# A Strassen feed-forward behind windowed attention: the written-out order of all engines, banks and buffers replaced by another one

## The chip, the cores and the metric

The kernel runs on one core of a Trainium2 chip. Its time is the device time of one launch in microseconds (us), and the median of several launches is what counts. TensorE is called PE here, its weight loads PEld, VectorE DVE, ScalarE ACT, GpSimd POOL and SyncE SP. POOL and SP do no arithmetic that matters in this kernel: POOL issues the loads, SP the stores and the transposes that the DMA engines make.

## The reference

Attention with a window of 96 keys and 8 global keys, biased by distance, feeds a two-layer network with a squared ReLU. There are 4 batches of 768 tokens, 8 heads of 64, and a hidden width of 2048.

```python
scores = scale * np.matmul(q, k.transpose(0, 1, 3, 2))
...
scores = np.where(keep, scores + bias[None], -1e9)
a = np.exp(scores - max); a = a / (sum(a) + 1e-09)
x = np.matmul(a, v).transpose(0, 2, 1, 3).reshape(B * S, H * D)   # 3072 x 512
h = x @ w_in                                                       # 512 x 2048
r = np.maximum(h, 0.0)
out = (r * r) @ w_out                                              # 2048 x 512
```

## The kernel before, in words

The 3072 tokens are 24 tiles of 128 (six to a batch), and two tiles make one of 12 blocks. A loop over tiles and a loop over blocks only describe operations: each gets a name, the engines it may run on, what it depends on and the function that emits it (class `Plan`). What is emitted, in which order, on which engine and in which memory, stands in a table of 1224 words, `ORDER`, which `Plan.run` walks from the first to the last. Each engine works through its own instructions strictly in the order of the table.

A word is a name, then possibly `@A` or `@V` (ACT or DVE, where the operation may run on either), `#2` (the second operation of that name), and after a colon the numbers, in hexadecimal, of the banks or buffers that it takes: the eight PSUM banks for an operation of PE, one of 16 buffers `buf` of 128x512 float32 for most others.

The names, with the line of the profile of the kernel before:

- `ld.q.1`, `ld.win.3.0`, `ld.wout.2`: the first 34 loads, all issued by POOL (L327); `load.9.1` loads queries and keys of tile 9 (two DMAs), `load.9.0` its values (one), by POOL too (L331). `gate.9` is a DVE memset of one column of a value buffer (L501), for which `load.9.0` waits, and which itself waits for the last readers of that buffer.
- `T.9`: the transpose of the queries and keys of tile 9, a DMA issued by SP (L557), from tile 8 on; for tiles 0 to 7 it is `tr` on PE (L531) and a copy `T`.
- `sc.9.0`: the scores (PE, L621, 16 matmuls; 8 for the first tile of a batch, 24 where two tiles share one operation). `exp` (ACT, L687), `mul` by the exponential of the bias (DVE, L712), `pv.9.0` and `pv.9.1` (PE, L774, 8 matmuls each, or 4), `norm.9` (DVE, a reciprocal at L808 and a product at L809, which writes `x`).
- `xT.9`: the transpose of `x`, a DMA issued by SP (L894) from tile 8 on, before that `trx` on PE and a copy.
- `xs.4.0` to `xs.4.2`: sums of quarters of `xT` of block 4 (DVE, L988). The first layer is a Strassen product, for each block and each half of the hidden width (`h.4.0`, `h.4.1`) seven products `p1` to `p7` of 8 matmuls (PE, L1019), with copies `u` out of PSUM in between (ACT at L450 or DVE), sums with ReLU `c` (DVE at L1064; `c21` is a plain ReLU, at L919 on ACT) and squares `q` (ACT at L1086 or DVE at L1088). Block 0 and half of block 1 are done the plain way (`s1`, L1140, `relu`, `sq`).
- `sum.4.0` to `sum.4.3`: sums of the squared hidden values (DVE, L1234). The second layer is again seven products for each block, `s2.4.p1.0` and so on, in pieces of 4 matmuls (PE, L1279), with copies `part` (ACT at L450 or DVE at L452), and `o` (DVE, L1354, or a copy), which fill an output buffer.
- `st.4.0`: the store of the first 128 rows of block 4 (SP, L1376).

Three queues set what can start when. PE runs its pieces in the order of the table, and each waits for its operands and for its bank to be read out. SP issues stores and transposes in the order of the table, so that a store stands still behind a transpose whose `norm` isn't done, whoever waits for the store's buffer. POOL issues loads in the order of the table in the same way: a load waits for the readers of the buffer that it fills, and all behind it wait too.

`Plan.run` does no more than this:

```python
for word in ORDER.split():
    word, _, banks = word.partition(":")
    name, _, letter = word.partition("@")
    name, _, nth = name.partition("#")
    o = byname[name][int(nth or 1) - 1]
    o["engine"] = self.ENGINES[letter] if letter else next(iter(o["engines"]))
    o["banks"] = [int(b, 16) for b in banks]
```

Of the kernel before, what the change touches and what calls it, by code (L numbers as in the profile page):

```python
# [57 lines left out]
tr.0.0:0 T.0.0@A E0.1 tr.1.0:1 T.1.0@A ld.k.1 tr.1.1:2 T.1.1 bias.1.0:0345 ld.q.1 tr.0.1:2 T.0.1 ld.q.2 ld.k.2  # L58
bias.0.0:16 tr.0.2:7 T.0.2@A sc.1.0 exp.1.1.1:0 sc.0.0 exp.0.1.0:1 exp.1.0.1 exp.0.0.0 exp.1.0.0:3 tr.1.2:7 T.1.2 ld.q.3
tr.0.3:2 ld.k.3 tr.1.3:7 T.0.3 gk.1 T.1.3 exp.1.1.0 ld.v.1 bias.2.0:2654 sc.2.0 exp.2.1.1:2 gk.2 ld.v.0 exp.2.0.1  # L60
exp.2.0.0:4 pv.1.0:01 pv.1.1 ones.6 norm.1:0 sc.3.0:3745 gk.3@A exp.3.1.1:0 ld.k.4 tr.1.4:2 ld.q.4 exp.3.0.0:3 T.1.4
tr.0.4:0 T.0.4 gv.1 exp.2.1.0 exp.3.1.0 pv.0.0:12 pv.0.1 norm.0:1 mul.3.0:1 exp.3.0.1 mul.3.1:5 sc.4.0:0536 exp.4.1.0:6
ld.v.2 pv.2.0:12 pv.2.1 gv.2 exp.4.0.1:3 exp.4.1.1 trx.0:4 ld.q.5 norm.2:1 gk.4 tr.0.5:7 T.0.5@A xT.0:0 trx.1:5 ld.k.5
tr.1.5:3 T.1.5@A mul.4.1:0 xT.1@A ld.v.3 pv.3.0:12 pv.3.1 norm.3:0 exp.4.0.0 mul.4.0:3 sc.5.0:3476 exp.5.0.1:5 exp.5.1.1
ld.win.1.0 trx.2:5 xT.2:1 ld.win.3.0 s1.0.1:0 trx.3:1 xT.3 gv.3 s1.0.1#2 relu.0.1:6 s1.0.3:6 s1.0.3#2 relu.0.3:1 E0.0
exp.5.1.0:2 s1.1.1:0 relu.1.1@V:4 ld.v.4 ld.win.6.0 ld.win.0.0 ld.win.0.1 pv.4.0:56 pv.4.1 ld.win.2.0 ld.win.2.1 ld.v.5
s1.0.6:4 exp.5.0.0 relu.0.6:0 s1.1.3:0 sq.0.1:0 mul.5.1:3 norm.4:0 s1.1.0:4 s1.0.0:5 ld.win.7.0 s1.0.2:6 ld.win.5.0
relu.1.0:6 relu.1.3:5 sq.0.3 s1.1.2:3 s1.0.0#2 gv.4 gate.9 mul.5.0:7 relu.1.2:2 isum.0.0 isum.1.0 isum.2.0 sq.1.1:1
xs.1.0:0 pv.5.0:01 trx.4:4 xT.4@A:2 sq.1.3 pv.5.1 norm.5:0 isum.3.0 s1.0.2#2 s1.0.0#3 s1.0.0#4 relu.0.0@V:5 xs.1.1
ld.win.4.0 isum.0.1 xs.1.2 s1.0.2#3 s1.0.2#4 s1.0.7:4 sq.1.0 h.2.0.p1:0 u.2.0.1:6 trx.5:5 xT.5 isum.1.1 isum.2.1  # L70
relu.0.2:4 relu.0.7:3 s1.0.5:1 sq.1.2 h.1.1.p1:3 u.1.1.1:7 h.1.1.p2:6 relu.0.5:2 gate.10 h.2.1.p2:4 h.2.1.p1:5 sq.0.0
h.1.1.p6 u.2.1.1:1 h.2.0.p2:1 s1.0.4:7 xs.2.0:1 xs.2.1 xs.2.2 gate.14 c.1.1.c11:8 sq.0.6 h.2.1.p6 ld.wout.1 u.1.1.2:7
relu.0.4:0 sq.0.2 u.2.1.2:5 h.2.0.p6 u.2.0.2:4 isum.3.1 h.1.1.p7 u.1.1.3:9 c.2.1.c11:a h.2.1.p5:7 ld.wout.3 ld.wout.0
ld.wout.2 wsum.0.0 c.2.0.c11:1 h.2.0.p5:4 h.2.1.p7 u.2.1.3:6 h.2.0.p7 wsum.1.0 wsum.3.0 h.1.1.p5:1 s2.0.p1.0:6 h.2.1.p4
s2.0.p2.0:2 c.2.1.c22:b h.1.1.p4 h.2.1.p3 sq.0.4 sq.0.5 c.1.1.c22:0 wsum.2.0 ld.wout.4 sq.0.7 sum.0.0:0 u.2.0.3:9
h.2.0.p4 c.2.0.c22:3 q.1.1.c11 c.2.1.c21:2 ld.wout.6 ld.wout.7 c.1.1.c21:8 ld.wout.5 s2.0.p1.1 c.2.0.c21:9 s2.0.p2.1
q.2.1.c21:2 q.1.1.c21 part.0.p1:0 s2.1.p2.0:3 h.1.1.p3 load.6.1 tr.1.6:0 wsum.0.1 tr.0.6:5 sum.0.1 wsum.1.1 c.2.1.c12:2
o.0.p2:8 h.2.0.p3 c.1.1.c12:5 s2.1.p2.1 sum.0.2 s2.0.p6.0 s2.0.p6.1 wsum.3.1 wsum.2.1 gate.11 c.2.0.c12:7 load.6.0
load.7.0 s2.0.p5.0 s2.0.p5.1 load.7.1 tr.0.7:1 tr.1.7:7 q.2.0.c22 q.2.1.c11 q.1.1.c22 part.0.p6:0 T.1.6@A s2.0.p7.0
s2.0.p7.1 s2.1.p1.0:0 s2.1.p1.1 q.2.1.c22 q.1.1.c12 sum.0.3 sum.1.0:1 q.2.0.c21 part.0.p7:1 o.0.p5:9 s2.0.p4.0 T.0.6@A  # L80
sum.1.1 q.2.1.c12 s2.0.p4.1 gate.12 o.0.p4@V part.1.p1:1 T.0.7@A load.8.1 q.2.0.c12 s2.0.p3.0 s2.0.p3.1 sum.1.2 o.0.p3
sum.2.0:0 sum.1.3 o.1.p2:7 T.1.7@A s2.1.p6.0 s2.1.p6.1 part.1.p6:0 sc.6.0:276154 s2.1.p7.0 load.9.1 q.2.0.c11 sum.2.1
exp.7.0.0:2 s2.1.p7.1 part.1.p7@V:1 exp.6.1.0:1 exp.6.0.0 mul.6.0:4 gk.7@A T.8 s2.1.p5.0 s2.1.p5.1 s2.1.p4.0 s2.1.p4.1
exp.7.1.0 mul.7.0:5 o.1.p5:1 exp.7.0.1:b exp.7.1.1 mul.7.1:2 sc.8.0:1276 exp.8.1.1:0 exp.8.0.0:a pv.6.0:45 pv.6.1
norm.6:0 exp.8.0.1 s2.1.p3.0 s2.1.p3.1 o.1.p3 sum.2.3 s2.2.p1.0:6 o.1.p4 pv.7.0:45 pv.7.1 norm.7:1 gk.8@A s2.2.p1.1
trx.6:0 xT.6:2 exp.8.1.0 mul.8.1:2 gv.7@A T.9 sc.9.0:2371 load.10.1 load.9.0 part.2.p1:0 s2.2.p6.0 trx.7:0 exp.9.1.0:5
s2.2.p6.1 xT.7 exp.9.0.1:b gk.9@A h.3.1.p1:3 u.3.1.1:0 part.2.p6:1 load.12.0 load.8.0 s2.2.p2.0:0 mul.8.0:4 pv.8.0:45
pv.8.1 h.3.0.p1:7 s2.2.p2.1 T.10 xs.3.0:1 xs.3.1 norm.8:1 xT.8:1 sum.2.2 exp.9.0.0 mul.9.0:2 h.3.1.p6 xs.3.2 o.2.p2:5
h.3.0.p2:4 exp.9.1.1 u.3.0.1:4 c.3.0.c11:a gv.8 h.3.0.p6 s2.2.p7.0 u.3.1.2:3 load.11.1 gate.16 s2.2.p7.1 h.3.1.p7
h.3.1.p5:4 u.3.0.2:6 h.3.0.p7 mul.9.1:4 u.3.1.3:c c.3.1.c22:b pv.9.0:12 pv.9.1 norm.9:0 u.3.0.3:d h.3.1.p4 q.3.0.c11:1  # L90
h.3.0.p4 c.3.0.c21:a q.3.0.c21 T.11 c.3.1.c21@V:4 h.3.1.p2:5 c.3.1.c11:c gv.9 h.3.1.p3 c.3.1.c12:a sc.10.0:3712
exp.10.1.1:0 exp.10.1.0:2 part.2.p7@V:0 h.3.0.p5:5 c.3.0.c22:3 s2.2.p5.0 s2.2.p5.1 o.2.p5:e h.4.1.p1:7 gate.13
exp.10.0.0 mul.10.0:d exp.10.0.1 mul.10.1:f q.3.1.c21 q.3.1.c11 h.3.0.p3 c.3.0.c12:4 s2.2.p3.0 load.10.0 pv.10.0:12
s2.2.p3.1 pv.10.1 norm.10:1 u.4.1.1:2 h.4.0.p1:3 s2.2.p4.0 gk.10@A s2.2.p4.1 sc.11.0:1254 gv.10 o.2.p3 q.3.0.c22 xT.9
q.3.1.c22 xs.4.0:1 xs.4.1 xs.4.2 q.3.0.c12 u.4.0.1:b q.3.1.c12 sum.3.2:0 sum.3.0 s2.3.p1.0:0 exp.11.0.0:4 exp.11.0.1:a
h.4.0.p6 exp.11.1.1 u.4.0.2:3 load.12.1 h.4.1.p6 s2.3.p1.1 h.4.0.p2:1 h.4.1.p2:5 c.4.0.c11:6 gate.17 u.4.1.2:f load.13.1
exp.11.1.0 h.4.1.p5:4 o.2.p4 h.4.0.p7 u.4.0.3:b st.1.1 T.12 part.3.p1:1 h.4.1.p7 u.4.1.3:1 h.4.0.p5:6 h.4.0.p4
c.4.0.c21:0 mul.11.1:c gate.15 mul.11.0:d sum.3.1 load.11.0 st.0.1 q.4.0.c21:2 pv.11.0:12 h.4.1.p4 c.4.0.c22:4 q.4.0.c22
c.4.1.c21:0 c.4.1.c22:d pv.11.1 s2.3.p6.0 norm.11:0 h.4.0.p3 s2.3.p6.1 part.3.p6:0 xT.10:2 T.13 c.4.0.c12:4 h.4.1.p3
gate.18 c.4.1.c12:3 q.4.1.c12 s2.3.p2.0:7 c.4.1.c11:1 s2.3.p2.1 s2.3.p7.0 s2.3.p7.1 q.4.1.c21 q.4.1.c11 o.3.p2:f  # L100
q.4.0.c11@V load.13.0 sc.12.0:546123 exp.12.1.0:1 s2.3.p5.0 s2.3.p5.1 exp.12.0.0 q.4.0.c12@V part.3.p7@V:1 s2.3.p4.0
exp.13.0.1:4 h.5.0.p2:5 sum.3.3 o.3.p5:6 mul.12.0:0 gk.13 exp.13.1.1 mul.13.1:3 st.1.0 xT.11 xs.5.0:1 xs.5.1 gate.20
exp.13.0.0:2 h.5.0.p1:2 u.5.0.1:1 exp.13.1.0 mul.13.0:4 s2.3.p4.1 pv.12.0:34 pv.12.1 norm.12:0 s2.3.p3.0 load.14.1 T.14
c.5.0.c11:2 xs.5.2 h.5.1.p1:6 h.5.0.p6 o.3.p4 u.5.1.1:0 u.5.0.2:7 s2.3.p3.1 o.3.p3 h.5.1.p6 load.15.1 T.15 xT.12:1
pv.13.0:01 h.5.0.p5:3 load.16.0 pv.13.1 norm.13:1 gv.13 u.5.1.2:c q.4.1.c22 h.5.0.p7 u.5.0.3:d c.5.0.c22:3 sum.4.0:0
sum.4.1 load.16.1 st.2.1 s2.4.p1.0:7 h.5.1.p7 u.5.1.3:1 s2.4.p1.1 part.4.p1:0 h.5.0.p4 c.5.0.c21:d sum.4.2 q.5.0.c21@V:1
sc.14.0:0154 exp.14.0.1:4 st.2.0 h.5.1.p4 gk.14 exp.14.1.0:b exp.14.1.1 exp.14.0.0 h.5.0.p3 c.5.0.c12:a h.5.1.p5:5
c.5.1.c22:e load.14.0 s2.4.p6.0 s2.4.p6.1 s2.4.p2.0:0 part.4.p6:1 c.5.1.c21:5 sc.15.0:3412 exp.15.0.1:1 exp.15.1.0:7
h.5.1.p3 h.5.1.p2:6 s2.4.p2.1 exp.15.1.1 mul.14.0:d mul.14.1:9 h.6.0.p2:4 c.5.1.c12:b pv.14.0:12 pv.14.1 gk.15@A T.16
s2.4.p7.0 s2.4.p7.1 o.4.p2:c s2.4.p5.0 c.5.1.c11:4 norm.14:0 q.5.0.c12 sc.16.0:1265 exp.15.0.0 mul.15.0:0 q.5.1.c12  # L110
load.17.1 part.4.p7:0 gate.22 q.5.1.c21 mul.15.1:b sum.4.3 xT.13 xs.6.0:1 exp.16.0.1:5 gv.14 xs.6.1 exp.16.0.0:1
exp.16.1.0 mul.16.0:7 s2.4.p5.1 o.4.p5:9 h.6.0.p1:3 h.6.1.p1:6 u.6.0.1:a c.6.0.c11:1 s2.4.p4.0 s2.4.p4.1 q.5.0.c22
# [1386 lines left out]
```

## Time and profile before

| what | value |
|---|---|
| three runs | 201.02, 201.80, 202.25 us; median 201.8 us |
| profiled execution | 202.63 us, of which the profile's span is 200.9 us |
| granted TensorE clock | 1.000 |
| DMA packets | 111713, 26.92 MB |
| first transposes by SP | issued from 49.1 us (queries and keys) and 63.6 us (`x`) on |
| last loads by POOL | issued at 138.2 us |

The span runs from the first to the last instruction that the profile shows; 1.7 us of the profiled execution lie outside. The profiled execution is 0.8 us above the median of the three runs. A row of the timeline gives start, length, engine, line, output and input, and in brackets how long the engine stood idle before and what ended it. In the chain of waits a DMA's row runs from its issue to its landing, and a row of PE from the start of its first matmul to the start of what comes next.

### The profile page before, as it was taken

Reading aid. Unit: us, or ns where it says so; the run is one execution under the profiler, and the core shown is the slowest. Engines: PE = TensorE matmul, PEld = TensorE weight load, DVE = VectorE, ACT = ScalarE, POOL = GpSimd, SP = SyncE. Lnnn points to the kernel's source line nnn. Section 1 sums busy time; section 2 is a strip of 40 time slices with the busy share of each in tenths; the row PEclk is TensorE's granted clock in tenths of the full one; section 3 lists DMA queues with packets and bytes.
Section 4 is the critical chain, followed back from the end, with each engine's and each line's share of the span. In section 5 each row is a group of like instructions: output and inputs, shape, how many; then the busy total and the mean of one; then the engine's idle time right before and its main releaser. Section 6 shows DMA issues by size and latency. Waiting matters only on the chain.

```text
span 200.9 us, 6834 instructions
## 1 busy us (share of the span) xinstructions
PE 189.5 (94%) x2808; PEld 170.2 (85%) x2808; DVE 175.5 (87%) x395; ACT 159.0 (79%) x331; POOL 75.3 (37%) x93
## 2 busy tenths in 40 slices
PE   7878999999999999999699998999998999999993
PEld 2666999999879989999589997998888989989882
DVE  8369899999999998999769996897998998999951
ACT  6699788999998699898399987658997698568320
POOL 8999774757458055428002922315000000000000
PEclk9999999999999999999999999999999999999999
...
GB/s 127 148 152 163 182 193 206 202 157 118 134 174 141 152 156 152 172 171 117 211 123 67 122 119 140 231 89 199 30 58 182 29 108 132 134 0 3 104 80 184
DMA packets 111713, 26.92 MB, mean 134 GB/s; under 512 B 103234, under 2 KB 108866, under 8 KB 111682
## 3 DMA queue, kind: packets, MB, share of 16 engines
...
## 4 chain that ended last, share of the span: by engine, by line
PE 49%; DMA 31%; POOL 7%; DVE 6%; ACT 2%; issue 2%; SPq 0%; DVEq 0%; POOLq 0%; ACTq 0%
PE bank L1279 24%; PE bank L1019 19%; DMA win<-in_moe_w_in_dram 8%; DMA xT<-x 6%; DMA wout<-in_moe_w_out_dram 5%; DMA out_dram<-buf 5%; POOL qk_first L327 4%; DMA qkT<-qk 3%; DMA qk<-in_k_dram 3%; PE bank L774 3%; PE bank L621 3%; POOL v L327 2%; DVE x L809 1%; ACT buf L450 1%; DVE hsum L1234 1%
## 5 line engine op out<-in xcount | busy, mean ns | idle before, releaser
L450 ACT COPY buf<-bank 128x512 f32<-128x512 f32 (+1 forms) x55 | 30.2, 569 | 14.1 <-PE bank L1019 6.5
L1279 PEld LDWEIGHTS <-hsum 128*128 128x128 bf16 x384 | 35.4, 98 | 4.4 <-DVE hsum L1234 0.4
L1279 PE MATMUL bank<-wsum,hsum 128*128 128x256 bf16 x288 | 38.0, 273 | 0.0
L1086 ACT ACTIVATE hs<-buf 128x512 bf16<-128x512 f32 x52 | 31.9, 639 | 4.9 <-DVE buf L1064 4.9
L1019 PEld LDWEIGHTS <-win 128*128 128x128 bf16 x504 | 30.9, 98 | 4.0 <-issue 3.1
L1019 PEld LDWEIGHTS <-qk_first 128*128 128x128 bf16 x504 | 30.8, 98 | 2.5 <-DVE xs L988 1.0
L687 ACT ACTIVATE buf<-bank 128x512 bf16<-128x512 f32 x56 | 31.2, 615 | 1.1 <-PE bank L621 0.9
L1064 DVE CUSTOM_DVE_ANT_0 buf<-bank,buf 128x512 f32<-128x512 f32 x41 | 28.0, 686 | 3.3 <-PE bank L1019 2.7
L1279 PEld LDWEIGHTS <-hs 128*128 128x128 bf16 x288 | 26.6, 98 | 3.0 <-issue 0.2
L1279 PE MATMUL bank<-wout,hs 128*128 128x256 bf16 x192 | 27.2, 273 | 0.0
L331 POOL DMA_DIRECT2D qk<-in_q_dram x18 | 15.9, 886 | 29.7 <-DMA qkT<-qk 24.8
L331 POOL DMA_DIRECT2D v<-in_v_dram x18 | 16.1, 897 | 28.1 <-PE bank L1279 14.6
L1019 PE MATMUL bank<-xT,win 128*128 128x128 bf16 x336 | 24.0, 219 | 2.4 <-ACT buf L919 1.6
L1019 PE MATMUL bank<-xs,qk_first 128*128 128x128 bf16 x336 | 24.2, 219 | 0.6 <-DVE xs L988 0.6
L687 ACT ACTIVATE early<-bank 128x512 bf16<-128x512 f32 x32 | 18.0, 604 | 1.0 <-PE bank L621 0.9
L809 DVE TENSOR_TENSOR x<-bank,rs 128x512 bf16<-128x512 f32 x24 | 16.6, 692 | 0.9
L331 POOL DMA_DIRECT2D qk<-in_k_dram x18 | 16.1, 894 | 1.6 <-DMA wout<-in_moe_w_out_dram 1.6
L1234 DVE TENSOR_TENSOR hsum<-hs 128x1024 bf16<-128x1024 bf16 (+1 forms) x26 | 16.4, 642 | 0.1
L1354 DVE TENSOR_TENSOR buf<-bank,part 128x256 f32<-128x256 f32 x32 | 13.2, 417 | 3.9 <-PE bank L1279 3.8
L450 ACT COPY part<-bank 128x256 f32<-128x256 f32 x30 | 11.2, 374 | 4.9 <-PE bank L1279 4.7
L919 ACT ACTIVATE buf<-bank 128x512 f32<-128x512 f32 x17 | 10.0, 608 | 4.9 <-DMA out_dram<-buf 2.8
L621 PEld LDWEIGHTS <-qkT 64*128 64x128 bf16 x352 | 10.1, 94 | 3.9 <-issue 2.5
...
## 6 DMA issues: line engine op xcount, KB each, us to landing
...
v<-in_v_dram POOLq DMA_DIRECT2D x24, 128.0 KB, 6.2
qk<-in_q_dram POOLq DMA_DIRECT2D x18, 128.0 KB, 5.5
qk<-in_k_dram POOLq DMA_DIRECT2D x18, 128.0 KB, 6.5
...
qk_first<-in_k_dram POOLq DMA_DIRECT2D x5, 128.0 KB, 4.7
```

The source lines that it names most:

```text
L327: ("ld",) + name, {"LD": t}, lambda e: nc.gpsimd.dma_start(out=dst, in_=src),
L331: nc.gpsimd.dma_start(out=dst, in_=src)
L450: nc.scalar.copy(dst, src)
L621: nc.tensor.matmul(out=tiles["sc", j, odd, g][:, at, :], lhsT=left[j - 1][half, pair, :] if kt else qkT[j % NKT][half, 1, pair, :], rhs=qk ...
L687: nc.scalar.activation(out=tiles[tag, j, g][:, odd], in_=tiles.pop(("sc", j, odd, g)).rearrange("p a c -> p (a c)"), func=Act.Exp, scale=s ...
L809: nc.vector.tensor_tensor(out=x.rearrange("p (b a) c -> p b a c", b=2), in0=po[:, :, :, :D], in1=rs.to_broadcast([P, 2, 4, D]), op=Alu.mult,)
L1019: nc.tensor.matmul(out=tiles["h", blk, g, bank][:, n], lhsT=left_[:, s, k], rhs=right_[:, k], start=opens and n == 0 and k == 0, stop=k == ...
L1064: nc.vector._custom_dve(TENSOR_ADD_SAT, out=hr, in0=src, in1=tiles.pop(("u", blk, g, i)), s0=float("inf"), s1=0.0,)
L1086: nc.scalar.activation(hs, hr, Act.Square)
L1234: nc.vector.tensor_tensor(out=t[:, i, h], in0=t[:, a, h] if isinstance(a, int) else half_a(blk, *a)[:, h], in1=t[:, b, h] if isinstance(b, ...
L1279: nc.tensor.matmul(out=tiles["acc", blk, bank][:, cols], lhsT=left_[:, s], rhs=right_[:, cols], start=first and s == 0, stop=s == NSTEP - ...
L1354: nc.vector.tensor_tensor(out=o_sb[:, cols], in0=tiles["acc", blk, bank][:, part], in1=tiles["part", blk, other][:, part], op=Alu.add,)
```

## The change

Only the table `ORDER` is replaced: the same 1224 words stand in another order, with other engines for some and other banks and buffers for most. It takes one line more, so that every line number of the kernel's body is one higher after the change. Nothing else in the file differs. Two lines of the diff, from the table's middle, stand for all of it:

```diff
-h.7.0.p2:4 c.7.0.c11:5 sum.6.0 u.8.0.1:d h.7.1.p4 c.7.1.c21:4 part.6.p1:0 h.8.1.p1:5 u.8.1.1:8 gate.21 xs.8.0:1 xs.8.1
...
+s2.5.p5.1 st.2.1 h.8.1.p1:2 q.7.0.c22 s2.5.p4.0 h.7.1.p3 o.6.p2:b gate.19 load.19.0 xs.8.0:1 xs.8.1 sum.6.1 u.8.1.1:e
```

On ACT, six `part` copies fewer stand (24 for 30) and five `xT` copies more (7 for 2); DVE has six `part` more and five `xT` fewer; the other exchanges are of at most five instructions each. Each engine's count of arithmetic is the same to within 10 instructions.

The first place is SP's queue around the two stores of block 2 (`out_dram<-buf`). `qkT` is written by the transposes of queries and keys, `xT` by those of `x`; the numbers are those of the buffers. Before, the two stores stand together behind `xT.12`, whose input `x_104` is made by `norm.12`:

```order
L557 DMA_TRANSPOSE qkT_85<-qk_69 128x8x128
L557 DMA_TRANSPOSE qkT_86<-qk_67 128x8x128
L894 DMA_TRANSPOSE xT_107<-x_104 128x4x128
L1376 DMA out_dram<-buf_127 128x512
L1376 DMA out_dram<-buf_118 128x512
L557 DMA_TRANSPOSE qkT_87<-qk_68 128x8x128
L894 DMA_TRANSPOSE xT_107<-x_105 128x4x128
```

After, from the transpose of tile 11's `x` on:

```order
L895 DMA_TRANSPOSE xT_108<-x_104 128x4x128
L558 DMA_TRANSPOSE qkT_86<-qk_67 128x8x128
L1377 DMA out_dram<-buf_116 128x512
L895 DMA_TRANSPOSE xT_107<-x_105 128x4x128
L558 DMA_TRANSPOSE qkT_87<-qk_68 128x8x128
L895 DMA_TRANSPOSE xT_107<-x_104 128x4x128
L558 DMA_TRANSPOSE qkT_88<-qk_69 128x8x128
L1377 DMA out_dram<-buf_125 128x512
```

One store of block 2 (`buf_116`) has moved ahead of `xT.12`; the other now stands 17 places further down, behind `xT.17`. The last row is a store of block 3.

The second place is DVE's queue from `norm.19` (the first row, which writes `x` of tile 19 into one of two buffers) to the first two sums of block 9 (the last two rows), which need the transposed `x` of tiles 18 and 19. L712 is `mul`, L1234 `sum`, L1354 `o`, L1088 `q`, L452 a copy. Before:

```order
L809 TENSOR_TENSOR x_104<-bank,rs 128x512
L712 TENSOR_TENSOR early<-early,E 128x1024
L1234 TENSOR_TENSOR hsum_114<-hs_110,hsum_114 128x1024
L1354 TENSOR_TENSOR early<-bank,part_132 128x256
L1234 TENSOR_TENSOR hsum_115<-hs_113 128x1024
L712 TENSOR_TENSOR buf_120<-buf_127,E 128x1024
L452 COPY qkT_83<-qkT_80 128x4x8
L1234 TENSOR_TENSOR hsum_115<-hsum_115,hs_113 128x1024
L988 TENSOR_TENSOR xs<-xT_106 128x2x256
L988 TENSOR_TENSOR xs<-xT_106,xs 128x256
```

After:

```order
L810 TENSOR_TENSOR x_105<-bank,rs 128x512
L713 TENSOR_TENSOR buf_117<-buf_119,E 128x1024
L1089 TENSOR_TENSOR hs_111<-buf_123 128x4x128
L453 COPY part_130<-bank 128x256
L1355 TENSOR_TENSOR buf_116<-bank,part_130 128x256
L713 TENSOR_TENSOR buf_119<-buf_128,E 128x1024
L1235 TENSOR_TENSOR hsum_115<-hs_111 128x1024
L713 TENSOR_TENSOR buf_128<-buf_123,E 128x1024
L989 TENSOR_TENSOR xs<-xT_106 128x2x256
L989 TENSOR_TENSOR xs<-xT_106,xs 128x256
```

Seven instructions stand between as before: four long ones, two short ones and a tiny copy have become five long and two short ones.

The third place is the end of POOL's queue, from the load of tile 19's values (`v_72`, the first row) on; that load waits for `gate.19`. `qk_67` to `qk_69` are the three buffers for queries and keys. Before:

```order
L331 DMA v_72<-in_v_dram 128x8x64
L331 DMA v_79<-in_v_dram 128x8x64
L331 DMA v_75<-in_v_dram 128x8x64
L331 DMA qk_69<-in_q_dram 128x8x64
L331 DMA qk_69<-in_k_dram 128x8x64
L331 DMA qk_68<-in_q_dram 128x8x64
L331 DMA qk_68<-in_k_dram 128x8x64
L331 DMA v_71<-in_v_dram 128x8x64
L331 DMA qk_67<-in_q_dram 128x8x64
L331 DMA qk_67<-in_k_dram 128x8x64
```

After:

```order
L332 DMA v_72<-in_v_dram 128x8x64
L332 DMA v_71<-in_v_dram 128x8x64
L332 DMA qk_68<-in_q_dram 128x8x64
L332 DMA qk_68<-in_k_dram 128x8x64
L332 DMA qk_67<-in_q_dram 128x8x64
L332 DMA qk_67<-in_k_dram 128x8x64
L332 DMA v_76<-in_v_dram 128x8x64
L332 DMA v_73<-in_v_dram 128x8x64
L332 DMA qk_69<-in_q_dram 128x8x64
L332 DMA qk_69<-in_k_dram 128x8x64
L332 DMA v_74<-in_v_dram 128x8x64
L332 DMA v_75<-in_v_dram 128x8x64
```

After, the queries and keys of tiles 19 and 20 stand ahead of that load and so are no longer in this piece; tile 21's (`qk_67`) stand fifth and sixth in it, where before they were ninth and tenth. `gate.19` itself has moved down DVE's queue: before, 93.8 us of PE's work stand ahead of it in the table, after the change 115.3 us. At the queue's front, the last four loads of `w_out` now stand behind tile 6's queries and keys, tile 8's ahead of tile 7's, and the values of tiles 6, 7 and 8, which were issued with them, behind tile 9's queries and keys.

More of the change, by code (lines that the diff above doesn't have):

```diff
@@ L57 @@
 ORDER = """
[L58 to L112, printed above, removed]
@@ new lines @@
+h.5.0.p5:3 q.5.1.c11:1 h.5.0.p4 s2.4.p2.0:0 gate.16 c.5.0.c22:f pv.14.0:56 pv.14.1 sum.4.2 norm.14:1 exp.15.1.0:5
+exp.15.0.0 gk.15@A s2.4.p2.1 sum.4.3 o.4.p2:3 h.5.0.p3 gv.14 c.5.0.c12:d s2.4.p7.0 q.5.0.c22 c.5.0.c21:1 mul.15.1:f
+q.5.1.c21 T.16 sc.16.0:5621 exp.16.1.0:6 s2.4.p7.1 part.4.p7@V:1 s2.4.p5.0 h.6.0.p1:6 exp.16.1.1:7 xT.13 exp.16.0.1
+h.6.1.p1:1 mul.15.0:8 s2.4.p5.1 o.4.p5:e load.17.1 T.17 xs.6.0:1 xs.6.1 s2.4.p4.0 pv.15.0:23 pv.15.1 norm.15:0
+h.6.0.p2:7 q.5.0.c21 exp.16.0.0 s2.4.p4.1 q.5.0.c12 u.6.1.1:5 gk.16@A xs.6.2 u.6.0.1:f c.6.0.c11:d h.6.1.p2:5
```

147 lines of the change are left out of this document (99 added, 48 removed).

## The prediction

> **What bounds the kernel now.** I read the page first, then busy times by stage, then what ended each engine's waits in the stages where PE falls back, then the chain of waits.
>
> ```profile
> span 200.9 us, 6834 instructions
> PE 189.5 (94%) x2808; PEld 170.2 (85%) x2808; DVE 175.5 (87%) x395; ACT 159.0 (79%) x331; POOL 75.3 (37%) x93
> ```
>
> PE is busy for 94% of the span, so its work, which the change leaves as it is, is the bound, and only its pauses can go: 200.9 - 189.5 = 11.4 us. By stage:
>
> ```profile
> 0.00:20.00 20.00, 16.11 (x235) 11.52 (x236) 13.93 (x52) 16.14 (x36) 19.01 (x27) 1.00 1.81 147
> ...
> 40.00:60.00 20.00, 19.70 (x266) 17.22 (x264) 19.72 (x41) 19.14 (x43) 11.35 (x14) 1.00 2.05 146
> ...
> 90.00:110.00 20.00, 17.75 (x293) 16.05 (x290) 17.27 (x40) 15.98 (x35) 5.29 (x7) 1.00 1.26 133
> 110.00:130.00 20.00, 19.12 (x312) 18.11 (x310) 17.33 (x36) 16.28 (x35) 9.06 (x12) 1.00 2.12 152
> ...
> 150.00:160.00 10.00, 9.45 (x168) 8.76 (x166) 8.97 (x21) 7.16 (x16) 0.00 (x0) 1.00 0.44 100
> ```
>
> (From the left: stage, its length, then busy time of PE, PEld, DVE, ACT, POOL, the granted clock, DMA.) The start costs PE 3.9 us, 40 to 60 us 0.3, 90 to 110 us 2.25, 110 to 130 us 0.9, 150 to 160 us 0.55. In the second of these rows DVE is full (19.72 of 20). The clock is 1.00 throughout. What stands behind the largest pause is in the timeline:
>
> ```profile
> 90.87 1.92 SPq L894 DMA_TRANSPOSE xT<-x  x1
> 92.88 1.01 SPq L1376 DMA_DIRECT2D out_dram<-buf  x2
> 97.86 0.69 DVE L1064 CUSTOM_DVE_ANT_0 buf<-bank,early 128x512 f32<-128x512 f32 x1 [0.96 <-DMA out_dram<-buf]
> 98.61 0.43 PEld L1019 LDWEIGHTS <-qk_first 128*128 128x128 bf16 x7 [0.66 <-issue]
> 100.13 0.60 ACT L919 ACTIVATE buf<-bank 128x512 f32<-128x512 f32 x1 [2.79 <-DMA out_dram<-buf]
> 100.78 0.43 PEld L1019 LDWEIGHTS <-win 128*128 128x128 bf16 x7 [1.69 <-issue]
> ```
>
> The two stores of block 2 are issued right after `xT.12` has been; DVE and then ACT stand still until they land, because they want to write into the stored buffers, and PE stands behind both, 0.66 + 1.69 = 2.35 us. The other pauses after the start have the same nature, a late DMA:
>
> ```profile
> 55.96 0.28 PEld L621 LDWEIGHTS <-qkT 64*128 64x128 bf16 x10 [0.55 <-DMA qkT<-qk]
> ...
> 122.92 0.43 PEld L1019 LDWEIGHTS <-win 128*128 128x128 bf16 x7 [1.05 <-issue]
> ...
> 151.84 0.43 DVE L988 TENSOR_TENSOR xs<-xT 128x512 bf16<-128x512 bf16 x1 [0.90 <-DMA xT<-x]
> 152.64 0.34 PEld L1019 LDWEIGHTS <-qk_first 128*128 128x128 bf16 x6 [0.83 <-DVE xs L988]
> ...
> 176.21 0.69 DVE L1064 CUSTOM_DVE_ANT_0 buf<-bank,buf 128x512 f32<-128x512 f32 x1 [0.16 <-DMA out_dram<-buf]
> ...
> 180.63 0.43 PEld L1019 LDWEIGHTS <-win 128*128 128x128 bf16 x7 [0.33 <-issue]
> ```
>
> They are `T.8` (0.55), `xT.16` (1.05), `xT.19` by way of `xs` (0.83) and the store of block 8 by way of `c` (0.33). The chain of waits gives their times from issue to landing, and PE's pieces:
>
> ```profile
> 42.52 6.51 DMA qk<-in_k_dram
> 49.11 6.80 DMA qkT<-qk
> ...
> 56.59 0.35 PE bank L774 x8
> ...
> 59.39 0.55 PE bank L621 x16
> ...
> 61.15 0.45 PE bank L1019 x8
> 61.59 0.44 PE bank L1279 x4
> 62.03 0.49 PE bank L774 x16
> ...
> 88.46 0.24 PE bank L774 x8
> ...
> 93.47 6.64 DMA out_dram<-buf
> ...
> 101.86 0.42 DVE buf L1354
> ...
> 102.96 0.22 DVE rs L808
> 103.20 0.69 DVE x L809
> 103.89 0.60 DVE early L712
> ...
> 111.22 0.34 DVE buf L1354
> ...
> 114.19 8.69 DMA xT<-x
> ...
> 147.59 4.15 DMA xT<-x
> ...
> 172.49 3.57 DMA out_dram<-buf
> ```
>
> From these I measure distances in the two tables: PE's work between the piece that makes a DMA possible and the first instruction that needs its landing, at 0.45 us for eight matmuls of the first layer, 0.44 for four of the second, 0.49 for a tile's `pv`, 0.55 for a tile's `sc`. Where such a distance is longer than the DMA's way, nothing waits.
>
> **The change, part by part.** Work and counts are the same, so only waits have a price.
>
> *Stores of block 2.* Before, the way from the last `pv` of tile 12 (88.46), which releases `xT.12`, to the landings is 9.4 us for the first store (97.86) and 93.47 + 6.64 - 88.46 = 11.65 us for the second. PE's work up to their first users is 10 x 0.45 + 4 x 0.44 + 0.49 + 0.55 = 7.3 us, and 1.4 us more for the second. So both wait, and PE loses 2.35 us. After, `st.2.0` stands behind `xT.11` with 11 pieces of the first layer, 15 of the second and about 2.1 us of others from `pv.11` to its buffer's next user, 13.6 us; `st.2.1` stands behind `xT.17` with 15 and 10 pieces, 11.2 us. These waits go: 2.35 us. What is late next is the store `st.3.0`, first behind `xT.15`: 13 x 0.45 + 5 x 0.44 + 0.49 + 0.55 = 9.1 us against 9.4. I take 0.3 us for it; the ends are 0 and the 2.35 of the same wait before.
>
> *`xT.16`.* PE's work from `pv.16` to `h.8.0.p1` was 13 x 0.45 + 6 x 0.44 + 0.49 = 9.0 us, and 1.05 were lacking; now it is 16 x 0.45 + 13 x 0.44 + 0.49 = 13.4. The 1.05 us go, with 3.4 to spare.
>
> *`xT.19`.* From `pv.19` to the first piece that reads `xs` it was 5.4 us (7 pieces of the second layer, 3 of the first, `sc`, `pv`), and is 5.8 (9, 3, `sc`). DVE has as much between `norm.19` and `xs.9.0` as before, and two instructions more ahead of `norm.19`. Of 0.83 us I let 0.5 go, between 0 and 0.83.
>
> *Block 8's store.* The 0.33 us go: `c.11.1.c11` now takes a buffer that no store has to free.
>
> *`T.8`, `T.9` and the loads around them.* How far apart POOL's loads are issued and how long transposes take to land, in the answers on `v` and on `qkT`:
>
> ```profile
> L331 POOL DMA_DIRECT2D v<-in_v_dram x18: 873/902/947, 36.2 to 136.5; - x18
> DMA to landing us min/median/max: 3.6/6.2/9.5
> ```
>
> ```profile
> DMA to landing us min/median/max: 3.2/5.3/9.0
> ```
>
> `T.8` was issued (49.11) when tile 8's keys had landed (42.52 + 6.51). Ahead of tile 8's queries and keys stood POOL's first 34 loads and 6 other rows; now it is the 34 and 3 others, so they come 3 x 0.9 = 2.7 us earlier. PE reaches `sc.8.0` 0.9 us of work earlier, and 0.55 were lacking: 1.25 us to spare, and the 0.55 go. `T.9` gains one row, 0.9 us, while its `sc` comes 0.2 + 0.55 us earlier; it showed no wait, but how little it had to spare the rows don't say. I take 0.3 us, with 0 and 0.55, `T.8`'s old wait, as ends. The values of tile 6 stand 9 rows further back, 8.1 us. They had 56.59 - (36.2 + 6.2) = 14.2 us to spare, so about 5 are left: nothing.
>
> [...]
>
> *The loads behind `gate.19`.* After the change, PE has 17.5 us of work between that gate and `sc.21.0`. In this time five rows of POOL (4.5 us), a load of keys and `T.21` have to pass:
>
> ```profile
> qk<-in_k_dram POOLq DMA_DIRECT2D x18, 128.0 KB, 6.5
> ```
>
> 4.5 + 6.5 + 5.3 = 16.3 us, 1.2 to spare at medians. `xT.18` (5.5 us of PE's work after `pv.18`, before 6.0) and `xT.22` (5.4, before 6.2) have less room too. For the three I take 0.4 us; the ends are 0 and, with the slowest transpose, 9.0 - 5.3 - 1.2 = 2.5.
>
> *The end.* `st.8.1` now stands behind the first store of block 11, and 3.1 us of PE's work later `o.11.p5` takes its buffer, while block 8's other store took 3.57 us to land. I take 0.3 us, from 0 to 0.5. The last pieces of PE, and the copy and the store after them, stand as before.
>
> *The start.* The same 34 loads, of the same sizes, stand in nearly the same order: nothing, give or take one row of POOL, 0.9 us.
>
> *Sum.* 2.35 + 1.05 + 0.5 + 0.33 + 0.55 = 4.8 us go, 0.3 + 0.3 + 0.4 + 0.3 = 1.3 us come: 3.5 us less. The profiled execution's 202.63 us (span 200.9 and 1.7 around it) becomes 199.1. It lies 0.8 us above the median of the runs, 201.8, which becomes 198.3.
>
> **The rivals.** *Half of it comes back as waits for DVE and ACT.* While PE stood, DVE caught up: from 90 to 110 us it was busy for 17.27 of 20 us, and with 2.35 us less it would be 98% full; from 150 to 160, 8.97 of 9.45. For it speaks that DVE's and ACT's work are the same in sum; against it, that from 40 to 60 us DVE was 99% full and PE lost only 0.3. If the gains in these two stages (2.85 us) are halved, 1.4 us come back: 199.7; if nearly all of it does, 201.
>
> *The loads behind `gate.19` are late.* POOL's whole end hangs on one DVE memset, with 12 rows behind it. If `T.21` needs its slowest 9.0 us and DVE comes to the gate 1 us late, PE waits 2.5 + 1.0 us instead of 0.4: 201.4. Against it speaks that few other loads are under way then.
>
> *DVE becomes the bound, and the kernel slower.* After the change DVE has, from the start of `sc.6.0` to that of `pv.8.0`, eight long instructions at 0.60 us, five short ones at 0.34, two `norm` at 0.22 + 0.69 and two tiny copies, 8.3 us, while PE has 8.8 us of work: 0.5 us of room in 9. The 0.60 and 0.34 are steps of the chain, where the next instruction starts before the one before it has ended; the lengths in the rows above are 0.69 and 0.42. If DVE has to wait for the end each time, it takes 8 x 0.09 + 5 x 0.08 = 1.1 us more, PE falls back by 0.6, and in nine blocks by 5.4: 203.7, and up to 207 where there is less room. For it speaks the full second row of the stages; against it that the steps were so short in the stage before, too. It decides once 3.5 us are lost, 0.4 in each block.
>
> *The change doesn't do what the tables show.* Excluded: there is no scheduler behind the table.
>
> **How the numbers follow.** The forecast, with its terms at other values of their ranges, has a chance of 0.54 and gives 196.5 to 199.7: at the low end 201.8 - 4.8, the 0.33 that `xT.19` may bring more, and 0.2 of the start's. The first rival has 0.2 (199.7 to 201, a fifth of it just below 199.8), the second 0.08 (about 201.4), the third 0.18 (203 to 207, a quarter of it below 203.8). A measurement of this kernel can tell about 1% from no change, here 2 us. So faster by over 1%, under 199.8: 0.54 + 0.04 = 0.58. Within 1%, up to 203.8: 0.16 + 0.08 + 0.04 = 0.28. Slower: 0.14. The range that is to hold the time 8 times in 10 leaves out most of the third rival and the lowest end: 196.6 to 203.0. The forecast's own is 196.5 to 199.7.
>
> **What would show it.** In the profile after, the rows of waits on `out_dram<-buf` between 90 and 125 us should be under 0.5 us together, and PE should hardly stand between 60 and 130 us; `T.8` and `xT.16` should land over 1 us before their users. If DVE stands for 0.5 us or more ahead of `xs` in block 9, or PE for `T.21`, the terms for these were too small. If PE waits for DVE or ACT in many places by 0.1 to 0.4 us, the first or third rival holds. The prediction is wrong if the start loses more than 4.8 us, or if PE's pauses after 20 us add up to more than 6 us.

## The result

| | median (lowest to highest), number of runs |
|---|---|
| before | 201.53 us (201.02 to 202.25), 4 |
| after | 199.30 us (198.62 to 201.74), 4 |
| before, later, on one chip with the next row | 201.23 us (197.83 to 207.06), 37 |
| after, later, same chip | 199.25 us (198.73 to 200.25), 12 |
| before, later, on the chip of `b_again`, `b_again2`, `b_st16` and `a_gate` | 200.99 us (199.08 to 202.94), 23 |
| before, later, on the chip of `a_back`, `a_part9`, `a_dve18` and `a_best` | 200.52 us (198.70 to 204.83), 29 |

The ratio of after to before is 0.9875, with a 95% interval from 0.983 to 0.992, that is 2.5 us less. The medians in the table differ by 2.2 us, and by 2.0 in the later series; 3.5 were forecast, and 199.3 us came where 198.3 was forecast. That ratio leaves out runs over 1.5% above the fastest of their kernel (one of after), which in the later series would drop 22 of the 37 runs of before on account of one run of 197.83 us and give 0.998 for the after and 0.992 for the moved stores, so medians of all runs are compared below. A difference of two such medians is known to about 0.8 us, by drawing the runs of each series anew at random: 2.0 for after may be 1.1 to 2.5.

### The profile page after: what moved, and what is told of

Its sections match the earlier page's. It is cut to its first block, busy times and chain, and to the rows that moved or that the text cites. A ratio compares the mean times of both kernels' runs of the same rounds, so it can differ in the third digit from the quotient of the medians.

```text
span 196.6 us, 6851 instructions
## 1 busy us (share of the span) xinstructions
PE 188.2 (96%) x2808; PEld 170.1 (86%) x2808; DVE 175.1 (89%) x396; ACT 161.2 (82%) x330; POOL 75.0 (38%) x93
## 4 chain that ended last, share of the span: by engine, by line
PE 83%; DVE 5%; DMA 4%; POOL 4%; issue 1%; ACT 0%; DVEq 0%; POOLq 0%
PE bank L1280 35%; PE bank L1020 32%; PE bank L1141 5%; PE bank L775 5%; PE bank L622 4%; POOL qk_first L328 3%; DMA v<-in_v_dram 2%; DMA xT<-x 2%; DVE x L810 1%; DVE buf L713 1%; PE bank L871 1%; PE bank L532 1%; DVE rs L809 1%; DVE v L453 1%; POOL v L328 0%
## 5 line engine op out<-in xcount | busy, mean ns | idle before, releaser
L1087 ACT ACTIVATE hs<-buf 128x512 bf16<-128x512 f32 x60 | 37.0, 648 | 6.5 <-DVE buf L1065 6.4
L688 ACT ACTIVATE buf<-bank 128x512 bf16<-128x512 f32 x72 | 40.0, 618 | 1.4 <-PE bank L622 1.0
L451 ACT COPY buf<-bank 128x512 f32<-128x512 f32 (+1 forms) x57 | 30.9, 564 | 11.5 <-PE bank L1020 6.1
L1065 DVE CUSTOM_DVE_ANT_0 buf<-bank,buf 128x512 f32<-128x512 f32 x46 | 31.0, 683 | 1.1 <-ACT buf L451 0.5
L713 DVE TENSOR_TENSOR buf<-buf,E 128x1024 bf16<-128x1024 bf16 x31 | 20.9, 681 | 1.1 <-ACT buf L688 1.1
L920 ACT ACTIVATE buf<-bank 128x512 f32<-128x512 f32 x22 | 13.1, 606 | 2.4 <-issue 1.0
L1355 DVE TENSOR_TENSOR buf<-bank,part 128x256 f32<-128x256 f32 x30 | 12.5, 419 | 1.8 <-PE bank L1280 1.7
L775 PE MATMUL bank<-v,buf 128*128 128x65 bf16 x296 | 13.4, 193 | 0.3 <-DVE v L453 0.3
```

Source lines behind the costliest of these rows:

```text
L451: nc.scalar.copy(dst, src)
L688: nc.scalar.activation(out=tiles[tag, j, g][:, odd], in_=tiles.pop(("sc", j, odd, g)).rearrange("p a c -> p (a c)"), func=Act.Exp, scale=s ...
L713: nc.vector.tensor_mul(at, tiles.pop(("esc", j, g)), bias)
L775: nc.tensor.matmul(out=po[:, hi, :], lhsT=tiles["at", j, g][:, odd, at * P : (at + 1) * P], rhs=v_sb[kj][:, h, :], start=(i == 0), stop=(i ...
L1065: nc.vector._custom_dve(TENSOR_ADD_SAT, out=hr, in0=src, in1=tiles.pop(("u", blk, g, i)), s0=float("inf"), s1=0.0,)
L1087: nc.scalar.activation(hs, hr, Act.Square)
```

## The profile after

The page of the kernel after the change:

```profile
span 196.6 us, 6851 instructions
...
PE 188.2 (96%) x2808; PEld 170.1 (86%) x2808; DVE 175.1 (89%) x396; ACT 161.2 (82%) x330; POOL 75.0 (38%) x93
```

The profiled execution took 198.62 us. By stage (length, then busy time of PE, PEld, DVE, ACT, POOL, the granted clock, the DMA engines' share; that share is the sum of the packets' times over the time of the 16 engines, so it can be above 1):

```profile
0.00:20.00 20.00, 15.28 (x220) 10.85 (x221) 12.63 (x44) 17.13 (x36) 19.18 (x28) 1.00 1.85 151
...
40.00:60.00 20.00, 19.92 (x273) 17.50 (x270) 19.31 (x42) 19.12 (x41) 11.40 (x13) 1.00 2.21 157
...
90.00:110.00 20.00, 20.00 (x351) 18.28 (x348) 19.13 (x44) 19.09 (x42) 6.13 (x7) 1.00 1.64 163
110.00:130.00 20.00, 20.00 (x299) 19.14 (x297) 19.33 (x43) 15.00 (x30) 4.38 (x6) 1.00 0.72 112
130.00:150.00 20.00, 19.95 (x295) 17.53 (x293) 19.07 (x41) 16.58 (x36) 6.11 (x7) 1.00 1.43 120
150.00:160.00 10.00, 9.92 (x166) 9.12 (x165) 9.55 (x19) 8.40 (x19) 0.00 (x0) 1.00 0.45 82
```

PE does not stand at all from 90 to 130 us, where it stood for 3.1 us, and from 20 to 180 us it stands for 0.25 us in all. The first 20 us cost it 4.72 us instead of 3.89. What it waits for, over the whole span (us in total, times, longest), are now things of the start:

```profile
PE bank L871 <- DVE x L810: 1.3, 2, 0.8
...
PE bank L622 <- DVE qkT L453: 0.5, 1, 0.5
PE bank L532 <- DMA qk_first<-in_k_dram: 0.5, 1, 0.5
PE bank L775 <- DMA v<-in_v_dram: 0.5, 1, 0.5
```

In the timeline, the two stores of block 2 (86.19 and 120.70, SP), the product on DVE that takes the first one's buffer (94.86), and what is left of the wait for tile 19's transpose (147.17 on DVE; at 147.98 PE's weight loads stand for 0.32 us, its matmuls for 0.05):

```profile
86.19 0.90 SPq L1377 DMA_DIRECT2D out_dram<-buf  x1
...
94.86 0.68 DVE L713 TENSOR_TENSOR buf<-buf,E 128x1024 bf16<-128x1024 bf16 x1
...
120.70 0.57 SPq L1377 DMA_DIRECT2D out_dram<-buf  x1
...
147.17 0.43 DVE L989 TENSOR_TENSOR xs<-xT 128x512 bf16<-128x512 bf16 x1 [0.25 <-DMA xT<-x]
...
147.98 0.45 PEld L1020 LDWEIGHTS <-qk_first 128*128 128x128 bf16 x8 [0.32 <-DVE xs L989]
```

The first store landed at 93.3, 1.5 us before DVE needed its buffer; `mul` starts there without a wait. `out_dram<-buf` is no longer among what DVE or ACT wait for between 60 and 190 us.

## The experiments

Theory 1 was the prediction's: PE's work is the bound and each wait has a price of its own. Theory 2: DVE and ACT use PE's pauses to catch up, so that about half comes back. Theory 3: DVE is the bound. Each edit is one of the table; the name of a kernel begins with `b` for the order before, `a` for the order after. Times are medians.

### The two orders again

`b_again` and `b_again2` are the order before, `a_again` is the order after, unchanged.

> The order before once more, unchanged, for a second profile: which of the pauses of 2.35 (stores of block 2), 1.05 (tile 16's x), 0.83 (tile 19's x), 0.33 (store of block 8) and 0.55 us (tile 8's queries and keys) come again. If they belong to the order, all five within 0.3 us. If some are chance of the execution that was profiled, those of the stores and of tile 19 stay and the others shrink, as they did beside the moved stores, where tile 8's transpose had 2.3 us to spare and tile 16's cost 0.2.

> The order before a third time, for one more profile. The same two readings: five pauses within 0.3 us of those shown, or the two of the stores and of tile 19 alone.

> The order after once more, unchanged, for its time beside the other runs on one chip and for a second profile. If the profiled execution shown is typical: PE's pauses in the first 20 us between 4.4 and 5.0 us, and under 0.6 us together from 20 to 180 us; the median of the runs 199.2, 2.3 below before. If the gaps of that profile are chance, they stand elsewhere.

The two executions of before took 202.82 and 200.14 us, with spans of 201.0 and 198.4. Their stages, `b_again` first:

```profile
90.00:110.00 20.00, 17.73 (x269) 15.86 (x267) 15.79 (x36) 14.64 (x31) 3.58 (x6) 0.91 1.71 121
110.00:130.00 20.00, 18.77 (x309) 17.81 (x307) 16.96 (x35) 16.11 (x35) 8.68 (x10) 1.00 2.15 150
...
150.00:160.00 10.00, 10.00 (x173) 9.32 (x171) 9.59 (x22) 7.30 (x17) 0.00 (x0) 1.00 0.54 105
```

```profile
90.00:110.00 20.00, 18.80 (x319) 16.93 (x316) 18.83 (x42) 17.11 (x38) 7.85 (x9) 1.00 1.16 130
110.00:130.00 20.00, 18.83 (x294) 17.95 (x293) 16.63 (x34) 15.94 (x34) 8.81 (x11) 1.00 1.83 155
...
150.00:160.00 10.00, 10.00 (x169) 9.24 (x167) 9.86 (x22) 7.76 (x17) 0.00 (x0) 1.00 0.51 118
```

In `b_again` the stores cost 2.27 us again and `xT.16` 1.23. In `b_again2` the stores landed in time (the later at 96.47), but tile 16's queries and keys came 1.2 us late instead, and `xT.16` cost 1.17. The pauses for `T.8`, `xT.19` and the store of block 8 are gone in both. In the profile that the prediction was made from they are 0.55, 0.83 and 0.33 us by PE's weight loads, which the prediction took, and 0.30, 0.55 and 0.15 by its matmuls. So two of the five pauses came again at their places, though not the stores' in every execution, and three were of that one execution. Neither reading of the expectations held: tile 19's went with the small ones, and tile 16's `x` stayed. From 20 to 180 us PE stood for 4.1, 3.5 and 2.5 us in the three profiles of before.

`a_again` (199.25 us) shows the same picture as the first profile of after, with 4.06 us of pauses in the first 20 us (4.4 to 5.0 were expected), and 0.5 from 20 to 180, nearly all of it at `xT.19`.

### The stores alone

```diff
-T.15 xT.12:1 ... load.16.1 st.2.1 ... exp.14.0.1:4 st.2.0
+T.15 st.2.1 st.2.0 xT.12:1 ... load.16.1 ... exp.14.0.1:4
```

> The order before, with one edit: the two stores of block 2 stand ahead of the transpose of tile 12's x instead of behind it. Theory 1 (PE's work is the bound, each wait has its own price): the 2.35 us that PE stood for these stores go, and the store's waits vanish from DVE's and ACT's rows between 97 and 101 us: 201.5 - 2.35 = 199.2. Theory 2 (DVE and ACT use PE's pauses to catch up): about half comes back as waits of 0.1 to 0.4 us: 200.3. Theory 3 (DVE is the bound): no change, 201.5.

It took 198.99 us (198.40 to 199.88, 12 runs) beside 201.23: 2.24 less. Theory 1 said 2.35. That it is met to 0.1 us is partly luck, since the difference may be 1.4 to 2.9 us; but theories 2 (1.2 less) and 3 (nothing) lie outside that, and fall at this place.

```profile
90.00:110.00 20.00, 19.69 (x339) 17.86 (x337) 19.57 (x43) 18.60 (x39) 9.09 (x11) 1.00 1.66 153
110.00:130.00 20.00, 19.99 (x306) 19.08 (x303) 17.68 (x35) 16.03 (x33) 7.28 (x9) 1.00 1.87 158
```

From 90 to 110 us DVE is now busy for 19.57 of 20 us and PE loses only 0.3 (to tile 17's queries and keys, which came 0.5 us late). `xT.16`, not touched, costs under 0.2 us here; why it shrank from 1.2, the runs don't show. Two words moved thus bring as much as the whole new order, and take most of the scatter away too.

### All five pauses, and the second one alone

`b_five` adds four edits to these stores, `b_st16` only the second of them:

```diff
-h.8.0.p1:1 h.7.1.p3 ... h.7.0.p4 load.22.0 s2.6.p1.1 s2.5.p5.1
+h.7.1.p3 ... h.7.0.p4 load.22.0 s2.6.p1.1 h.8.0.p1:1 s2.5.p5.1
...
-q.8.0.c21 h.9.1.p6 h.9.0.p6 s2.7.p3.1 part.8.p1@V:3 s2.8.p6.0
+q.8.0.c21 s2.7.p3.1 part.8.p1@V:3 s2.8.p6.0 h.9.1.p6 h.9.0.p6
...
-s2.9.p1.1 part.9.p1:1 s2.8.p3.1 o.8.p3 st.8.0
+s2.8.p3.1 o.8.p3 s2.9.p1.1 part.9.p1:1 st.8.0
...
-load.6.1 ... load.6.0 ... load.7.0 ... load.7.1 ... load.8.1
+load.6.1 load.7.1 load.8.1 ... load.6.0 ... load.7.0
```

> The order before, with five small edits, one for each pause that was named: the stores of block 2 ahead of tile 12's transpose; the first product of block 8 three pieces of PE later (tile 16's transpose); two products of block 9 two pieces later (tile 19's); block 8's last output piece one piece earlier (its store); tile 7's and 8's queries and keys ahead of the values of tiles 6 and 7 (tile 8's transpose). Theory 1: the pauses of 2.35, 1.05, 0.83, 0.33 and 0.55 us go, 5.1 together: 201.5 - 5.1 = 196.4. Theory 2: half comes back: 199.0. Theory 3: not below 200.5.

> The order before with the two moved stores, and the first product of block 8 three pieces of PE later (the second of the five edits alone). If the wait for tile 16's x has a price of its own, up to 0.2 us (what PE showed there beside the moved stores) less than 199.0: 198.8. If moving a piece on PE out of the way of a wait only sets up later waits, and that is where the five edits lost 0.95 us: 199.3 to 199.9.

`b_five` took 199.94 us: 0.95 more than the stores alone (it may be 0.3 to 1.8), 3.5 more than theory 1 said and 0.9 more than theory 2. Three of the five pauses were of one execution, so the four added edits had little to gain in any case. `b_st16` took 199.27 (beside a before of 200.99 on its chip), within the noise of the stores alone, so it can't tell whether the wait for tile 16's `x` still had a price of 0.2 us. PE's waits in `b_five` from 105 to 155 us, each behind what it waited for:

```profile
124.87 0.59 ACT L450 COPY buf<-bank 128x512 f32<-128x512 f32 x1 [1.45 <-DMA out_dram<-buf]
...
125.51 0.61 PE L1019 MATMUL bank<-xs,qk_first 128*128 128x128 bf16 x8 [0.23 <-ACT buf L450]
...
149.50 0.41 DVE L452 COPY part<-bank 128x256 f32<-128x256 f32 x1
...
149.96 0.60 PE L1279 MATMUL bank<-wsum,hsum 128*128 128x256 bf16 x4 [0.55 <-DVE part L452]
...
151.68 0.61 PE L1019 MATMUL bank<-xs,plain 128*128 128x128 bf16 x8 [0.23 <-ACT buf L450]
```

beside the one large one of `b_stores` in block 9:

```profile
148.72 1.07 PE L1019 MATMUL bank<-xs,qk_first 128*128 128x128 bf16 x16 [0.53 <-DVE xs L988]
```

The product that waited for `xs` has gone, and so has the wait for the transpose: DVE starts its sums `xs` at 147.95 without standing for it. PE now stands 0.55 us for a copy on DVE, `part.8.p1`, whose bank the next piece of PE needs. That piece has moved up on PE, but on DVE the copy still stands behind those sums and `norm.20` and ends at 149.91. The two smaller waits are for copies on ACT, and the first of these copies had itself waited 1.45 us for a store, a wait of 0.21 us in `b_stores`. From 20 to 180 us PE stands for 1.33 us in `b_five` and 0.85 in `b_stores`, in the first 20 us for 3.98 and 3.58, which together is about the 0.95 us, by one profile each. So a piece that moves on PE alone can set up a wait for another engine's queue; which of the four edits costs what, these runs don't separate.

### The late store put back

```diff
-T.15 st.2.0 xT.12:1 exp.14.1.0 mul.14.1:3
+T.15 xT.12:1 st.2.0 exp.14.1.0 mul.14.1:3
```

> The order after, with one word moved: the first store of block 2 stands behind the transpose of tile 12's x again, as before the change, instead of one place ahead of it. It will be issued at about 90.6 us instead of 86.2 and land 7 us later, at 97.7, while the product on DVE that takes its buffer starts at 94.9: DVE stands for 2.8 us. Theory 1 (a late store is what the kernel before paid for): PE stands for about 2 us there, 199.2 + 2.0 = 201.2, and the runs scatter more than after's. Theory 2 (the order after has slack in DVE that takes it up): within 0.5 us of after, 199.2 to 199.7.

199.29 us (198.86 to 201.19), where `a_again` took 199.25 on another chip; across chips 0.6 us can't be told. PE does not stand at all from 90 to 110 us in its profile (20.00 us busy), so nothing was lost at this place. The store was issued as expected, but was not late:

```profile
90.49 1.17 SPq L1377 DMA_DIRECT2D out_dram<-buf  x1
...
94.81 0.69 DVE L713 TENSOR_TENSOR buf<-buf,E 128x1024 bf16<-128x1024 bf16 x1
```

It landed at 94.72, 4.2 us after its issue instead of 7.1, 0.1 us before DVE took the buffer. The price that was expected was wrong, and the experiment doesn't tell the theories apart: the store was never late, so a late store's price is shown in the order before only. It shows that a store issued 4.3 us later landed only 1.4 us later.

### More work for DVE

```diff
-part.4.p6:2 ... part.5.p1:2 ... q.6.0.c12 ... q.7.0.c12
+part.4.p6@V:2 ... part.5.p1@V:2 ... q.6.0.c12@V ... q.7.0.c12@V
```

> The order after, with nine copies of the second layer's products (blocks 4 to 8) moved from ACT to DVE, at their places: 9 x 0.42 = 3.8 us more for DVE at most (3.1 by the steps of 0.34), as much less for ACT. From 60 to 180 us DVE is idle for 7.2 us after the change. Theory 1 (DVE has this room, PE stays the bound): less than 1 us more, 199.2 to 200.2. Theory 3 (DVE is the bound already): all of it, 202.3 to 203.0.

> As the kernel with nine copies moved, and nine squares of the first layer (blocks 4 to 9, 0.60 to 0.68 us each) moved from ACT to DVE too: 8.5 to 9.9 us more for DVE between 60 and 180 us, where 7.2 are idle. Theory 1: what exceeds the room is paid, 1.3 to 2.7 us, and some more where the room lies in other stages: 201 to 203. Theory 3: 207.7 to 209.

With nine copies moved 201.17 us (200.46 to 202.12), with nine squares as well 206.40 (206.17 to 206.65): 1.9 and 7.1 us more than `a_back` on the same chip. (In the edit, the first two words of each line stand for the nine copies, the last two for the nine squares.) The pages, nine copies first:

```profile
PE 190.4 (95%) x2808; PEld 171.2 (86%) x2808; DVE 177.5 (89%) x405; ACT 158.9 (80%) x321; POOL 75.1 (38%) x93
```

```profile
PE 192.8 (94%) x2808; PEld 171.6 (84%) x2808; DVE 183.0 (89%) x414; ACT 154.7 (76%) x312; POOL 75.0 (37%) x93
```

DVE's busy time rose by 2.4 and 7.9 us above the 175.1 of after, and the time rose by 0.8 to 0.9 us for each of them. Its share stays at 89% in all three. Theory 3's amounts were a little too large, and theory 1's far too small: the 7 us in which DVE is idle between 60 and 180 us are not room. They lie at waits for PE, ACT and transposes. What is paid may be DVE's added time, or that the moved copies end later on a full DVE, so that PE gets their banks back later: the runs don't tell these apart.

### The start and the end of POOL's queue

`a_start` has the start as it stood before in front of the new order, except that three words take other buffers at the seam and one, `ones.6`, stands later; `a_gate` moves the gate of tile 19's values over seven pieces of PE, 3.1 us of its work:

```diff
-gate.19 load.19.0 xs.8.0:1 xs.8.1 ... h.8.0.p7
+xs.8.0:1 xs.8.1 ... h.8.0.p7 gate.19 load.19.0
```

> The order after, with the start as it stood before the change: the first 107 words in the old order, banks and buffers, so that loads, transposes and scores of tiles 0 to 5 run as before, and the new order from there on. PE stood 4.72 us in the first 20 us after the change and 3.89 before. If the order of the start makes the difference: 0.8 us less than after (199.2), 198.4, and about 3.9 us of pauses in the first 20 us. If it is chance of one execution: as after, 199.2.

> The order after, with the gate of tile 19's values and their load eight pieces of PE later (3.1 us of its work), which holds back all of POOL's last twelve loads. Tile 21's transpose landed 0.5 and 1.1 us ahead of its user in two profiles. If it comes 3.1 us later, PE stands there for 2.0 to 2.6 us: 201.3 to 201.9. If transfers that start later land faster, as the late store did (4.2 us instead of 7.1): 200 or less.

`a_start` took 200.16 us, 0.9 more than `a_again`. Its first 20 us cost PE 3.66 us, but at the seam the products of tile 4 with v wait for ACT, which has the new order's work ahead of it:

```profile
24.35 0.52 PEld L775 LDWEIGHTS <-buf 128*128 128x128 bf16 x15 [1.35 <-issue]
```

So it doesn't tell whether the new start is worse. Over all profiles, the start as it stood after the change cost from 3.57 to 4.72 us in seven executions (mean 4.1), the one before from 3.22 to 3.98 in six (mean 3.7). About 0.3 us may be the order; that stays open.

`a_gate` took 200.10 us, 0.85 more than `a_again` (on another chip), between the two readings. The execution that was profiled took 202.3, far above the median, so only the place itself is read from it:

```profile
146.75 0.45 PEld L622 LDWEIGHTS <-qkT 64*128 64x128 bf16 x16 [1.32 <-DMA qkT<-qk]
```

PE stands 1.3 us for `T.21`: the gate does decide there once 0.5 to 1.1 us of spare are used up.

### A version that fills the wait instead

```diff
-mul.21.0:f xs.9.0:1 xs.9.1 ... exp.21.1.1 h.9.0.p6 gv.19@A ... pv.20.0:34 pv.20.1 ... mul.21.1:e sum.8.1
+mul.21.0:f sum.8.1 xs.9.0:1 xs.9.1 ... exp.21.1.1 gv.19@A ... pv.20.0:34 pv.20.1 h.9.0.p6 ... mul.21.1:e
```

> The order after, with two words moved around the wait for tile 19's transpose: on DVE a sum of block 8 that is ready stands ahead of the sums that wait for the transpose and fills their wait of 0.6 us; on PE tile 20's products with v stand ahead of the first product that needs these sums. If a wait is worth what PE shows, when both the queue that waits and PE get other work: PE's pauses of 0.2 to 0.6 at 147 and 0.25 at 153 us go, 0.5 to 0.8 us less than after, 198.5. If the pause only moves on to a later place: 199.2.

198.61 us (198.41 to 201.20, 11 of 12 runs under 199.4) beside 199.29 of `a_back` on the same chip: 0.7 less (it may be 0.2 to 1.1), as theory 1 has it, and 1.9 less than before on this chip; the after itself was not run there. The waits in `a_best`, and then those of `a_back`, where the transpose took about as long (4.7 and 4.6 us):

```profile
148.01 0.43 DVE L989 TENSOR_TENSOR xs<-xT 128x512 bf16<-128x512 bf16 x1 [0.40 <-DMA xT<-x]
...
148.82 1.05 PE L1020 MATMUL bank<-xs,qk_first 128*128 128x128 bf16 x16 [0.30 <-DVE xs L989]
```

```profile
147.76 0.43 DVE L989 TENSOR_TENSOR xs<-xT 128x512 bf16<-128x512 bf16 x1 [0.89 <-DMA xT<-x]
...
148.57 0.62 PE L1020 MATMUL bank<-xs,qk_first 128*128 128x128 bf16 x8 [0.69 <-DVE xs L989]
```

Not the transpose came sooner, but DVE did a sum while it waited, and PE tile 20's products: 0.5 us of DVE's wait and 0.4 of PE's are gone. `b_five` moved PE's pieces alone at the same place of the order before, and had waits of 0.55 and 0.23 us there instead of 0.53. The two words of `a_best` were not tried one by one, so how much is due to DVE's sum isn't known.

## Why the prediction was right, and where it was not

*The stores of block 2* (2.35 us). Right, in mechanism and size: moved alone, they bring 2.24 us. After the change the first had 1.5 us to spare and the second 3.9. `st.3.0`, for which 0.3 us were taken, had 4.1 to spare: it was issued at 106.9 us and landed in 3.3. What `out_dram<-buf` cost in the order before came in two of its three profiles, 2.35 and 2.27 us; in the third these stores landed in time.

*`xT.16`* (1.05). The wait is real (0.88, 1.23 and 1.17 us of PE's time in three profiles) and is gone: it lands 9.2 us before its user, 2.4 us after its issue instead of 8.7. The distance was to give 3.4 us of the 9.2; the rest is the transfer. That was overlooked: before, POOL issued ten loads from 109.2 to 121.0 us, and five were under way when `xT.16` was issued; now they wait behind `gate.19` until 125.6, and none is. That the loads made the difference no run isolates. Whether the wait has a price of its own stays open. With the stores moved it shrank to under 0.2 us by itself, and taking that away too brought nothing that could be told from noise; but in `b_again2`, where the stores cost nothing, it was there with 1.17 us.

*`xT.19`, block 8's store and `T.8`* (0.5, 0.33 and 0.55). The terms that were miscounted are these, together with the last step of the sum. They were pauses of one execution, absent in two others, so an average execution could not give them back. And that execution was 1.1 us above the median of four runs: the sum took its extra pauses off as gains, and then took its excess of 0.8 us off once more to come to the median, as if it lay elsewhere. The 1.4 us are counted wrongly. At `xT.19` the order after has a wait of its own: DVE stood for 0.25 and 0.62 us there in two profiles of after, and 0.89 in `a_back`. By the prediction's own sign (0.5 us or more ahead of `xs`) this term was wrong in two of the three. The other signs held: no waits for `out_dram<-buf` from 90 to 125 us, PE hardly standing from 60 to 130 us, `T.8` 1.8 and `xT.16` 9.2 us ahead of their users.

*What was to come* (1.3). Hardly any of it did at the places named. `T.9` had 4.1 us to spare, `o.11.p5` 0.8, `T.21` 0.5 (1.2 were estimated), `xT.18` 0.4. The values of tile 6 had 2.8 us left instead of 5, because POOL stood 3.0 us for the buffer of tile 9's queries and keys, now ahead of them; that was overlooked, and cost nothing. In all, 3.0 of the 4.8 us that were to go went, and 0.8 of the 1.3 that were to come came, at other places: that the time came out within 1 us of the forecast is in part luck, since the two errors pull opposite ways.

*The start and the end* (nothing). By the two profiles of after and the three of before, the first 20 us cost PE 0.5 us more, part of it chance, and the end 0.3: from 180 us to the end of the span PE stands for 3.6 us instead of 3.3. Nine stores are now issued within the last 6 us of PE's work, and the DMA share there is 0.8 to 1.0, where before it was 0.2 to 0.4 until the last 2 us.

So the account of the means of these five profiles is: 3.4 us of pauses between 20 and 180 us become 0.4, which is 3.0 less, and 0.5 and 0.3 come at the two ends: 2.2 less, as the medians have it. The agreement is partly luck. The spans of these profiles differ by 3.2 us (200.1 and 196.9 in the mean); the other 1.0 is PE's busy time, 189.6 and 188.5, of which about half is, by an estimate, the lowered clock of `b_again` (3.4 us at 0.50 in one of three executions, below). And by all profiles of either start, the first 20 us cost 0.3 us more, not 0.5.

*The rivals.* The first, half comes back through DVE and ACT, fell at the stores, where DVE filled up and PE lost at most 0.3 us more. In `b_five` a wait for a copy on DVE and two for copies on ACT did come up in place of others, but there pieces of PE had been moved. The second didn't occur, by 0.5 us. The third was nearer than the prediction took it: work moved to DVE is paid at 0.8 to 0.9 of its length, so DVE has hardly any room beside PE. It didn't strike because the change adds nothing to DVE (175.5 and 175.1 us busy). Its price, longer steps between instructions, didn't appear: around 95 us, DVE's long instructions still start 0.60 us apart.
